# Two VectorE operations planned one unit later, and one copy out of PSUM shared by two engines

## The chip, the cores and the metric

The kernel runs on one NeuronCore of one Trainium2 chip. Times are device microseconds (us) of that core. Before the change the kernel takes 263.32 us, the median of 7 runs (263.03 to 264.03).

The engines are TensorE (PE in the profile; PEld are its weight loads), VectorE (DVE), ScalarE (ACT), GpSimd (POOL) and SyncE (SP, which here only issues DMAs). Each engine works through its own instructions strictly in order and waits at an instruction until what it needs has been signalled. PSUM is the matmul's output memory, in eight banks of 512 fp32 columns by 128 partitions.

## The reference

For each of 8 batches and 8 heads, with sequence 576 and head dimension 64:

```
q_s = exp(q) / sum over d of exp(q)          # softmax over the head dimension
k_s = exp(k) / sum over s of exp(k)          # softmax over the sequence
kv  = k_s^T v                                # 64 x 64 per head
x   = q_s kv                                 # heads side by side: 4608 tokens x 512
h   = x w_in                                 # 4608 x 2048
out = (h * sigmoid(h)) w_out                 # 4608 x 512, fp32
```

The inputs are q, k, v (8 x 8 x 576 x 64) and w_in (512 x 2048), w_out (2048 x 512), all fp32. The reference also subtracts a maximum before each exp and adds 1e-9 to each sum.

## The kernel before

**Tiling.** The 4608 tokens are cut into nine chunks `t` of 512 tokens. Attention is done batch by batch (576 tokens). As 576 is 512 and 64 more, batch 0 fills chunk 0 and the first 64 columns of chunk 1, batch 1 gives the other 448 columns of chunk 1 and the start of chunk 2, and so on. `pieces(t)` says which columns of which batch make up a chunk; for chunk 1 the columns that are still to be made begin at 64, hence the shapes 128x448 and 128x896 (two of them) in the profile.

**Attention of a batch `b`.** ScalarE takes the exp of q (`exp_q`, line 108) and of k (`exp_k`, line 113), in two calls each, one per two pairs of heads. VectorE sums exp(q) over the head dimension and takes the reciprocal (`qsum`, lines 154 to 158: with an argument `gs` it sums one group of heads per call, and the reciprocal follows the second). GpSimd or VectorE multiplies by it (`qnorm`, line 163). The normalised q is transposed, by TensorE for batches 0 and 1 and by a DMA on SP's queue (`q_transpose`, line 173) from batch 2 on. `vcast` turns v into bf16 with a column of ones (line 91 or 89). `kv` (line 195) multiplies k and v on TensorE into banks 6 and 7, `kvcopy` (lines 206 and 208) normalises the result on VectorE into `kvn`, and `xt` makes x transposed from it: `xt_mm` (line 234) writes banks 6 and 7 (bank `6 + s` for the head `s` of a pair of heads), and `xt_evac` copies both banks to the fp16 tile `XTS[t % 2]`, by one instruction on the engine that it is given. `xt(t, 0)` and `xt(t, 1)` use the same two banks one after the other. The helper `copy` (lines 89 and 91) records all copies.

**First matmul (x w_in).** Chunk 0 is done plainly. In chunk 1, eight of sixteen blocks of 128 features, and in chunks 2 to 8 all of them, are done in groups with seven half-size products in place of eight (Strassen's scheme in Winograd's form): `group(t, g, i)` for i in the order 1, 2, 6, 5, 7, 4, 3, line 377. Each product needs sums or differences of halves of the weights (`ws_op`, line 328, on VectorE, into `WS`) or of x (`xs_op`, line 338, on VectorE, into `XS1` to `XS4`). After products 1, 6 and 7 the banks 0 and 1 are copied out as `h` (`group_snap`, line 89 or 91), and after 2, 7 and 3 VectorE adds the other pair of banks to such a copy (`group_add`, line 355). That other pair is 6 and 7 in chunk 1, and 2 and 3 in later chunks. Products 2, 5 and 3 write it: 5 begins anew in the banks after the add of 2 has read them, and 3 adds to what 5 left after the add of 7 has read them. `group_silu` (line 361) on ScalarE makes `GT`, the input of the second matmul.

**Second matmul (g w_out).** Chunk 0 is done plainly (`mm2_plain`, line 414, into banks 2 to 5). Chunks 1 to 8 use the same seven-product scheme (`prod`, line 477), with `T1` to `T4` made once from w_out by `t_op` (line 461) on VectorE, and with sums of `GT` made for each chunk by `s_op` (line 451) on VectorE. `s_op(t, i, f0, f1)` does the part of the blocks f0 to f1.

**Order.** The order is written out by hand. The list `units` holds TensorE's work, one piece after the other; `plan(u, f)` puts `f` ahead of unit `u`. What is emitted ahead of a unit, or by the unit itself after its matmuls (a snapshot, an add), enters each engine's own queue in this order, so an operation moved past a unit moves past what that unit emits for the same engine. Functions planned for the same unit are emitted in the order of the `plan` calls. Units that the change touches:

- `b1` is the first unit after chunk 0's first matmul. Units `b1` to `b1 + 8` are `mm2_plain(0, 0)` to `mm2_plain(0, 8)`. Then, to `b1 + 22`, seven products of `group(1, 1, i)` and the other seven `mm2_plain` mix: product 1 is unit `b1 + 9`, product 2 is `b1 + 11`, product 6 is `b1 + 12`, product 5 is `b1 + 14`, product 7 is `b1 + 16`, product 4 is `b1 + 19` and product 3 is `b1 + 21`. Units `b1 + 23` to `b1 + 30` are plain blocks of chunk 1 (`mm1`, line 285). Batch 2's attention is planned between these: its q by `exp_q(2, ...)`, `qsum(2, ...)` and `qnorm(2, ...)`, then the k-v product at `b1 + 25` and x at `b1 + 27` and `b1 + 29`.
- `begin[NCH]` is the first unit of the last chunk's second matmul. The 28 units before it mix the last chunk's first matmul with chunk 7's second one; unit `begin[NCH] - 7` is product 7 of the last group, `- 6` a product of chunk 7's second matmul, `- 2` product 3 of the last group.

Of the kernel before, what the change touches and what calls it, by code (L numbers as in the profile page):

```python
# [17 lines left out]
def kernel(  # L18
# [9 lines left out]
    nc = tc.nc  # L28
# [9 lines left out]
    TCH = 512  # L38
    HT = TCH // 2
    HN = DM // 2  # L40
    NCH = NT // TCH
# [24 lines left out]
    XTS = [glob.tile([128, NC, S], FP16, name=f"XT{i}") for i in range(2)]  # L66
# [7 lines left out]
    PS = ps.tile([128, 8, 512], FP32, name="PS")  # L74
# [12 lines left out]
    def copy(eng, o, i):  # L87
        if eng is nc.scalar:
            eng.copy(out=o, in_=i)  # L89
        else:  # L90
            eng.tensor_copy(o, i)  # L91
# [10 lines left out]
    def half(t, cc):  # L102
        return t[:, :, cc * 128:(cc + 1) * 128].rearrange("p j (g d) -> p j g d", d=D)

    def exp_q(b, cc, g0=0, g1=2):
        if "eq" not in st[b]:
            st[b]["eq"] = ap.tile([128, J, NG * D], BF16, name="eq")
        nc.scalar.activation(  # L108
            out=half(st[b]["eq"], cc)[:, :, g0:g1], in_=jgd(b, "qt", cc)[:, :, g0:g1], func=ACT.Exp
        )  # L110
# [34 lines left out]
    def new_zq(b):  # L145
        if "zq" not in st[b]:
            st[b]["zq"] = ap.tile([128, 2, J, 2], FP32, name="zq", bufs=2)
            st[b]["rzq"] = ap.tile([128, 2, J, 2], FP32, name="rzq", bufs=2)

    def qsum(b, cc, gs=None):  # L150
        new_zq(b)
        z, e = st[b]["zq"][:, cc], half(st[b]["eq"], cc)
        if gs is None:
            nc.vector.reduce_sum(out=z, in_=e, axis=AX.X)  # L154
        else:
            nc.vector.reduce_sum(out=z[:, :, gs], in_=e[:, :, gs, :], axis=AX.X)  # L156
        if gs != 0:
            nc.vector.reciprocal(out=st[b]["rzq"][:, cc], in_=z)  # L158

    def qnorm(b, cc, eng):  # L160
        e = half(st[b]["eq"], cc)
        r = st[b]["rzq"][:, cc]
        eng.tensor_tensor(  # L163
            out=e, in0=e, in1=r[:, :, :, None].to_broadcast([128, J, 2, D]), op=ALU.mult
        )
# [49 lines left out]
    def kv_both(b):  # L215
        kv(b, 0)
        kv(b, 1)
        kvcopy(b)

    def pieces(t):  # L220
        a, e = (S, 2 * TCH) if t == 1 else (t * TCH, (t + 1) * TCH)
        got = []
        while a < e:
            b, col = divmod(a, S)
            n = min(S - col, e - a)
            got.append((b, col, n, a - t * TCH))
            a += n
        return got

    def xt_mm(b, cc, col, n, bank, dst):  # L230
        for r in range(2):
            for s in range(2):
                h = slice(s * 64, (s + 1) * 64)
                nc.tensor.matmul(  # L234
                    out=PS[r * 64:(r + 1) * 64, bank + s, dst:dst + n],
                    lhsT=kvn[b % 3][h, cc, r, :],
                    rhs=st[b]["qT"][h, col // P:(col + n) // P, cc, r * 64:(r + 1) * 64],
                )

    def xt_evac(t, cc, bank, d0, d1, o0, eng):  # L240
        o = XTS[t % 2][:, 2 * cc:2 * cc + 2, o0:o0 + d1 - d0]
        copy(eng, o, PS[:, bank:bank + 2, d0:d1])

    def xt(t, cc, eng=nc.scalar):
        got = pieces(t)
        for b, col, n, dst in got:
            xt_mm(b, cc, col, n, 6, dst)
        xt_evac(t, cc, 6, got[0][3], TCH, got[0][3], eng)


    def silu(t, fb, i, o, w):
# [68 lines left out]
    def ws_op(i, g):  # L320
        w, f0, f1 = WS[g], 4 * g + 8, 4 * g
        in0, in1, op = {
            1: (wa(0, f1), wa(1, f1), ALU.add),
            2: (w[0], wa(0, f0), ALU.subtract),
            3: (wa(0, f0), wa(0, f1), ALU.subtract),
            4: (wa(1, f0), w[1], ALU.subtract),
        }[i]
        nc.vector.tensor_tensor(out=w[i - 1], in0=in0, in1=in1, op=op)

    def xs_op(t, i):  # L330
        x = [xs[:, :, 0:width(t)] for xs in XS4]
        in0, in1 = {
            1: (xb(t, 0, 1), xb(t, 0, 0)),
            2: (xb(t, 1, 1), x[0]),
            3: (xb(t, 1, 1), xb(t, 0, 1)),
            4: (xb(t, 1, 0), x[1]),
        }[i]
        nc.vector.tensor_tensor(out=x[i - 1], in0=in0, in1=in1, op=ALU.subtract)
# [100 lines left out]
    def blk(t, kh, th):  # L439
        return GTS[t % 2][:, kh * HF:(kh + 1) * HF, th * HT:(th + 1) * HT]  # L440

    def s_op(t, i, f0=0, f1=HF):
        in0, in1, op = {
            1: (blk(t, 0, 1), blk(t, 1, 1), ALU.add),
            2: (SS[1], blk(t, 0, 0), ALU.subtract),
            3: (blk(t, 0, 0), blk(t, 0, 1), ALU.subtract),
            4: (blk(t, 1, 0), SS[2], ALU.subtract),
        }[i]
        f = slice(f0, f1)
        o = blk(t, 0, 1) if i == 3 else SS[i]  # L450
        nc.vector.tensor_tensor(out=o[:, f], in0=in0[:, f], in1=in1[:, f], op=op)

    def t_op(i, eng, f0=0, f1=HF):
        o, in0, in1 = {
            1: (T1, B12, B11),
            2: (T2, B22, T1),
            3: (T3, B22, B12),
            4: (T4, B21, T2),
        }[i]
        f = slice(f0, f1)  # L460
        eng.tensor_tensor(out=o[:, f], in0=in0[:, f], in1=in1[:, f], op=ALU.subtract)
# [161 lines left out]
    def plan(u, f):  # L623
        at.setdefault(u, []).append(f)
# [7 lines left out]
    begin = {1: len(units)}  # L632
# [25 lines left out]
    def full(t):  # L658
# [27 lines left out]
        plan(u + 17, lambda: q_transpose(b))  # L686
        plan(u + 15, lambda: kv_both(b))
        plan(u + 22, lambda: xt(t + 1, 0, nc.vector))
        plan(u + 27, lambda: xt(t + 1, 1))
        plan(u, lambda: (xs_op(t, 1), xs_op(t, 2), xs_op(t, 3), xs_op(t, 4)))  # L690

    for t in range(2, NCH):
        if t < B - 1:
            full(t)
            continue
        begin[t] = u = len(units)
        bs = b_units(t - 1, ORDER)
        gs = [lambda t=t, g=g, i=i: group(t, g, i) for g in (1, 0) for i in ORDER]
        plan(u + 2, lambda t=t: s_op(t - 1, 1))
        plan(u + 4, lambda t=t: s_op(t - 1, 2))  # L700
        plan(u + 5, lambda t=t: s_op(t - 1, 3))
        plan(u + 21, lambda t=t: s_op(t - 1, 4))
        for x in 2 * four_pairs:
            units.append({"b": bs, "g": gs}[x].pop(0))
            if x == "g" and len(gs) % 7 == 0:
                later = 1 if t == NCH - 1 and not gs else 3
                f0 = 12 if gs else 8
                plan(len(units) - 1 + later, lambda t=t, f0=f0: group_silu(t, 1, f0, 1))
        assert not (bs or gs)
        plan(u, lambda t=t: (xs_op(t, 1), xs_op(t, 2), xs_op(t, 3), xs_op(t, 4)))  # L710
        if t < NCH - 1:
            plan(u + 23, lambda t=t: xt(t + 1, 0, nc.vector))
            plan(u + 26, lambda t=t: xt(t + 1, 1))
# [2 lines left out]
    begin[NCH] = len(units)  # L716
    last = NCH - 1
    plan(begin[NCH] - 11, lambda: s_op(last, 1, 4, 8))
    plan(begin[NCH] - 7, lambda: s_op(last, 2, 4, 8))
    plan(begin[NCH], lambda: (s_op(last, 1, 0, 4), s_op(last, 2, 0, 4), s_op(last, 3)))  # L720
    plan(begin[NCH] + 6, lambda: s_op(last, 4))

# [48 lines left out]
    b1 = begin[1]  # L771
# [16 lines left out]
    plan(b1 + 5, lambda: (vcast(1, 1, nc.scalar, 0, 1), vcast(1, 1, nc.vector, 1, 2)))  # L788
    plan(b1 + 6, lambda: (trcopy(1, 1, 0, 5, 0, nc.scalar), trcopy(1, 1, 5, J, 1)))
    plan(b1 + 7, lambda: kv_both(1))  # L790
    plan(b1 + 8, lambda: xt(1, 0))
    plan(b1 + 9, lambda: xt(1, 1))

    plan(b1 + 3, lambda: (ws_op(1, 1), ws_op(2, 1)))
    plan(b1 + 4, lambda: ws_op(3, 1))
    plan(b1 + 6, lambda: ws_op(4, 1))
    plan(b1 + 8, lambda: t_op(1, nc.vector))
    plan(b1 + 10, lambda: (xs_op(1, 1), ws_op(1, 0)))
    plan(b1 + 10, lambda: (xs_op(1, 2), xs_op(1, 3), xs_op(1, 4)))
    plan(b1 + 10, lambda: exp_q(2, 0))  # L800
    plan(b1 + 11, lambda: (qsum(2, 0, 0), qsum(2, 0, 1), qnorm(2, 0, nc.gpsimd)))
    plan(b1 + 13, lambda: exp_q(2, 1))
    plan(b1 + 14, lambda: exp_k(2, 0))
    plan(b1 + 14, lambda: (qsum(2, 1, 0), qsum(2, 1, 1), qnorm(2, 1, nc.gpsimd)))
# [56 lines left out]
```

## Time and profile before

| | |
|---|---|
| median of 7 runs | 263.32 us |
| profiled execution, whole | 264.22 us |
| its span, first to last instruction | 262.4 us |
| mean granted TensorE clock | 0.997 |
| TensorE matmuls busy | 251.6 us, 96% of the span |
| VectorE busy | 208.9 us, 80% |
| ScalarE busy | 187.5 us, 71% |
| GpSimd busy | 65.6 us, 25% |
| HBM traffic | 36.70 MB read, 9.44 MB written |

The profile is one execution, recorded by the hardware profiler. A row of the timeline gives the start from the span's start, the length, the engine, the line of the program and the operation with output and input; in brackets, where there is one, the idle time of the engine before it and what ended it. An instruction's recorded end reaches a little into the next one of the same engine, since their parts overlap; matmuls follow each other before the earlier one's recorded end, a 512-column one 0.216 us after its predecessor's start. The chain of waits goes back from the last instruction to whatever released each step.

In this program chunk 0's first matmul ends at about 32.5 us, units `b1` to `b1 + 30` take until about 64 us, seven stretches of about 26 us for chunks 2 to 8 follow, and the second matmul of the last chunk begins at about 245 us.

### The profile page before, as it was taken

What the parts mean: (1) busy time and instruction counts of PE and PEld (TensorE: products, weight loads), DVE (VectorE), ACT (ScalarE), POOL (GpSimd) and SP (SyncE); (2) the same over time, 40 slices, a digit from 0 to 9 for tenths busy, and PEclk for the clock granted to TensorE, in tenths of its full rate; (3) what the DMA queues carried; (4) which work ended last, traced back from release to release, by engine and by line L of the source; (5) the groups of instructions that cost most, each with busy time, mean ns of one, the idle gap of its engine ahead of it and who ended that gap; (6) DMA issues with size and microseconds to landing.
All of it is one profiled execution on the core that took longest, in us unless ns stands there. A gap on an engine that the chain in (4) does not pass through costs nothing.

```text
span 262.4 us, 6409 instructions
## 1 busy us (share of the span) xinstructions
PE 251.6 (96%) x2732; PEld 203.2 (77%) x2732; DVE 208.9 (80%) x268; ACT 187.5 (71%) x212; POOL 65.6 (25%) x63
## 2 busy tenths in 40 slices
PE   8799899799999999999999999999999999999992
PEld 3367656465888888888888888888888888888881
DVE  2867797999897999799979997999798548855832
ACT  4765887698996699669966995699574748484610
POOL 1643691370270306030603060306000000000003
PEclk9999999999999999999999999999999999999998
DMA  6999999659999587857784879540434003400624
GB/s 248 338 188 296 300 326 330 242 97 354 332 332 215 159 213 253 163 167 170 295 202 133 207 254 181 155 98 2 90 71 92 2 0 72 91 2 1 139 64 120
DMA packets 35964, 45.89 MB, mean 175 GB/s; under 512 B 16208, under 2 KB 21008, under 8 KB 35936
## 3 DMA queue, kind: packets, MB, share of 16 engines
q1 hardware_dynamic: 29568, 33.69, 47.1%
q0 software_dynamic: 6128, 11.60, 17.2%
q8 instruction: 21, 0.34, 0.5%
q10 hardware_dynamic: 240, 0.20, 0.2%
q14 instruction: 7, 0.06, 0.1%
HBM read 36.70 MB, written 9.44 MB: 176 GB/s over the span
## 4 chain that ended last, share of the span: by engine, by line
PE 83%; DMA 5%; issue 4%; POOL 2%; ACT 2%; DVE 2%; POOLq 0%; ACTq 0%
PE PS L477 36%; PE PS L377 34%; DMA qt<-in_q_dram 5%; PE PS L414 5%; PE PS L285 2%; PE PS L234 2%; PE PS L195 2%; POOL W L554 1%; PE PS L267 1%; POOL out_dram L740 1%; ACT eq L108 1%; DVE zq L156 1%; ACT sg L256 0%; PE PS L181 0%; DVE h L355 0%
## 5 line engine op out<-in xcount | busy, mean ns | idle before, releaser
L355 DVE TENSOR_TENSOR h<-PS,h 128x1024 f32<-128x1024 f32 (+1 forms) x45 | 53.9, 1198 | 12.2 <-ACT h L89 6.3
L477 PEld LDWEIGHTS <-GT 128*128 128x128 f16 x512 | 49.6, 98 | 6.9 <-issue 1.2
L377 PEld LDWEIGHTS <-WS 128*128 128x128 f16 x480 | 46.8, 98 | 7.9 <-issue 2.3
L477 PE MATMUL PS<-W,GT 128*128 128x256 f16 x384 | 49.1, 273 | 0.0
L377 PE MATMUL PS<-XS,WS 128*128 128x256 f16 (+1 forms) x360 | 46.3, 272 | 1.5 <-DVE h L355 1.5
L361 ACT ACTIVATE GT<-h 128x1024 f16<-128x1024 f32 (+1 forms) x45 | 46.1, 1047 | 0.3 <-DVE h L355 0.3
L89 ACT COPY h<-PS 128x1024 f32<-128x1024 f32 (+1 forms) x35 | 35.1, 1004 | 14.7 <-PE PS L377 14.3
L477 PEld LDWEIGHTS <-S 128*128 128x128 f16 x384 | 37.1, 98 | 5.2 <-issue 1.0
L163 POOL TENSOR_TENSOR eq<-eq,rzq 128x1152 bf16<-128x1152 bf16 x13 | 27.5, 2116 | 54.6 <-DVE rzq L158 51.9
L377 PEld LDWEIGHTS <-W 128*128 128x128 f16 x360 | 34.7, 98 | 4.7 <-issue 0.2
L477 PE MATMUL PS<-T,S 128*128 128x256 f16 x256 | 32.7, 273 | 0.0
L377 PE MATMUL PS<-XT,W 128*128 128x256 f16 (+1 forms) x240 | 29.5, 272 | 0.0
L361 ACT ACTIVATE GT<-PS 128x1024 f16<-128x1024 f32 (+1 forms) x15 | 15.3, 1017 | 18.9 <-PE PS L377 18.9
L91 POOL CAST vaug<-vt 128x1152 bf16<-128x1152 f32 x12 | 14.8, 1240 | 45.1 <-DMA vt<-in_v_dram 37.1
L108 ACT ACTIVATE eq<-qt 128x1152 bf16<-128x1152 f32 (+1 forms) x18 | 19.1, 1059 | 3.5 <-DMA qt<-in_q_dram 3.4
L740 POOL DMA_DIRECT2D out_dram<-ow x5 | 2.7, 546 | 72.5 <-DVE ow L725 72.5
L113 ACT ACTIVATE ek<-kt 128x1152 bf16<-128x1152 f32 x16 | 18.4, 1154 | 1.5 <-DMA kt<-in_k_dram 1.5
L154 DVE TENSOR_REDUCE zq<-eq 128x18 f32<-128x1152 bf16 x12 | 16.1, 1345 | 4.0 <-ACT eq L108 4.0
L267 PE MATMUL PS<-XT,W 128*128 128x288 f16 x128 | 16.2, 286 | 1.1 <-DVE GT L257 0.8
L477 PE MATMUL PS<-W,S 128*128 128x256 f16 x128 | 16.5, 273 | 0.0
L497 DVE SCALAR_TENSOR_TENSOR ow<-PS,sc 128x512 f32<-128x512 f32 x7 | 4.8, 692 | 14.5 <-ACT sc L493 14.5
L267 PEld LDWEIGHTS <-W 128*128 128x128 f16 x128 | 12.4, 98 | 4.9 <-issue 1.2
(79 smaller groups left out, 347.7 us busy)
## 6 DMA issues: line engine op xcount, KB each, us to landing
out_dram<-ow SPq DMA_DIRECT2D x64, 128.0 KB, 2.4
qt<-in_q_dram SPq DMA_DIRECT2D x12, 576.0 KB, 4.6
kt<-in_k_dram SPq DMA_DIRECT2D x12, 576.0 KB, 5.7
vt<-in_v_dram SPq DMA_DIRECT2D x12, 576.0 KB, 5.5
qt<-in_q_dram POOLq DMA_DIRECT2D x4, 576.0 KB, 10.8
kt<-in_k_dram POOLq DMA_DIRECT2D x4, 576.0 KB, 13.8
vt<-in_v_dram POOLq DMA_DIRECT2D x4, 576.0 KB, 12.6
W<-in_moe_w_out_dram POOLq DMA_DIRECT2D x4, 512.0 KB, 14.9
```

The costliest lines, as they stand in the source:

```text
L89: eng.copy(out=o, in_=i)
L91: eng.tensor_copy(o, i)
L108: nc.scalar.activation(out=half(st[b]["eq"], cc)[:, :, g0:g1], in_=jgd(b, "qt", cc)[:, :, g0:g1], func=ACT.Exp)
L113: nc.scalar.activation(out=half(ek, cc), in_=jgd(b, "kt", cc), func=ACT.Exp)
L154: nc.vector.reduce_sum(out=z, in_=e, axis=AX.X)
L163: eng.tensor_tensor(out=e, in0=e, in1=r[:, :, :, None].to_broadcast([128, J, 2, D]), op=ALU.mult)
L267: nc.tensor.matmul(out=PS[:, WIDE[fb] + n, 0:S // 2], lhsT=W1[:, c, fb * 128:(fb + 1) * 128], rhs=XTS[0][:, c, n * (S // 2):(n + 1) * (S / ...
L355: nc.vector.tensor_tensor(out=four(t, i), in0=group_bank(t, True), in1=four(t, i), op=ALU.add)
L361: nc.scalar.activation(out=group_out(t, f, n), in_=x, func=ACT.Silu, scale=1.0 / XS)
L377: nc.tensor.matmul(out=PS[:, bank + p // 2, (p % 2) * HT:(p % 2) * HT + width(t)], lhsT=a[:, c, p * 128:(p + 1) * 128], rhs=bb[:, c, 0:wid ...
L414: nc.tensor.matmul(out=PS[:, 2 + tb, :], lhsT=GTS[t % 2][:, fc, tb * 128:(tb + 1) * 128], rhs=W2[:, fc, :], start=(fc == 0), stop=(fc == N ...
L477: nc.tensor.matmul(out=PS[:, bank, m * HN:(m + 1) * HN], lhsT=a[:, fc, m * 128:(m + 1) * 128], rhs=bb[:, fc, :], start=(first and fc == 0) ...
```

## The change

There are three edits.

- `xt(1, 0)`, batch 1's x for the first two pairs of heads, is copied out of PSUM by two instructions: ScalarE takes bank 6 and VectorE bank 7, 128x448 each, where ScalarE took both, 128x896, in one. `t_op(1)`, the first sum of w_out's quarters (`T1`), was planned for `b1 + 8` after `xt(1, 0)` and is now planned for `b1 + 9`; in VectorE's queue it comes after the new copy.
- `qsum(2, 0, 0)` and `qsum(2, 0, 1)` on VectorE, with the reciprocal, and the following `qnorm(2, 0)` on GpSimd are planned for `b1 + 12` in place of `b1 + 11`. Unit `b1 + 11` is product 2, which emits its add for VectorE; the sums come behind it now.
- `s_op(last, 2, 4, 8)` is planned for `begin[NCH] - 6` in place of `- 7`. Unit `begin[NCH] - 7` is product 7 of the last group, which emits its add for VectorE; the subtraction comes behind it now.

```diff
@@ -245,7 +245,12 @@
         got = pieces(t)
         for b, col, n, dst in got:
             xt_mm(b, cc, col, n, 6, dst)
-        xt_evac(t, cc, 6, got[0][3], TCH, got[0][3], eng)
+        if eng is None:
+            o0 = got[0][3]
+            for s, e in enumerate((nc.scalar, nc.vector)):
+                copy(e, XTS[t % 2][:, 2 * cc + s, o0:TCH], PS[:, 6 + s, o0:TCH])
+        else:
+            xt_evac(t, cc, 6, got[0][3], TCH, got[0][3], eng)
@@ -716,7 +721,7 @@
     begin[NCH] = len(units)
     last = NCH - 1
     plan(begin[NCH] - 11, lambda: s_op(last, 1, 4, 8))
-    plan(begin[NCH] - 7, lambda: s_op(last, 2, 4, 8))
+    plan(begin[NCH] - 6, lambda: s_op(last, 2, 4, 8))
@@ -788,17 +793,16 @@
     plan(b1 + 7, lambda: kv_both(1))
-    plan(b1 + 8, lambda: xt(1, 0))
-    plan(b1 + 9, lambda: xt(1, 1))
+    plan(b1 + 8, lambda: xt(1, 0, None))
+    plan(b1 + 9, lambda: (t_op(1, nc.vector), xt(1, 1)))
 
     plan(b1 + 3, lambda: (ws_op(1, 1), ws_op(2, 1)))
     plan(b1 + 4, lambda: ws_op(3, 1))
     plan(b1 + 6, lambda: ws_op(4, 1))
-    plan(b1 + 8, lambda: t_op(1, nc.vector))
     plan(b1 + 10, lambda: (xs_op(1, 1), ws_op(1, 0)))
     plan(b1 + 10, lambda: (xs_op(1, 2), xs_op(1, 3), xs_op(1, 4)))
     plan(b1 + 10, lambda: exp_q(2, 0))
-    plan(b1 + 11, lambda: (qsum(2, 0, 0), qsum(2, 0, 1), qnorm(2, 0, nc.gpsimd)))
+    plan(b1 + 12, lambda: (qsum(2, 0, 0), qsum(2, 0, 1), qnorm(2, 0, nc.gpsimd)))
     plan(b1 + 13, lambda: exp_q(2, 1))
```

## The prediction

> **What bounds the kernel now.** I read the page first, then the list of who waited for whom in the stage of batch 1 (39 to 66 us), then the chain of waits and the timeline there, and the timeline of the last 25 us. On the page the thing to see is that TensorE holds the chain; only time during which TensorE stands still is to be won.
>
> ```profile
> span 262.4 us, 6409 instructions
> ...
> PE 251.6 (96%) x2732; PEld 203.2 (77%) x2732; DVE 208.9 (80%) x268; ACT 187.5 (71%) x212; POOL 65.6 (25%) x63
> ...
> PE 83%; DMA 5%; issue 4%; POOL 2%; ACT 2%; DVE 2%; POOLq 0%; ACTq 0%
> ```
>
> The list of TensorE's waits from 39 to 66 us has one row, of waits, times and the longest:
>
> ```profile
> PE PS L377 <- DVE h L355: 1.5, 1, 1.5
> ```
>
> The chain of waits (start, length, what) says how VectorE's add came to be late: ScalarE's exp of batch 2's q, then the sums `qsum` over it on VectorE, then the reciprocal, and only then the add that frees banks 6 and 7.
>
> ```profile
> 44.89 1.18 ACT eq L108
> 46.07 0.02 issue
> 46.09 1.43 DVE zq L156 x2
> 47.52 0.02 issue
> 47.54 0.27 DVE rzq L158
> 47.80 0.96 DVE h L355
> 48.76 0.04 issue
> 48.80 0.93 PE PS L377 x8
> ```
>
> In the timeline (start, length, engine, line), note that the matmuls before the stall start at 46.23, and that an fp16 subtraction on VectorE which meets a running GpSimd operation takes far longer than its kind elsewhere:
>
> ```profile
> 46.23 1.03 PE L414 MATMUL PS<-W,GT 128*128 128x512 f16 x4
> ...
> 47.72 1.03 DVE L355 TENSOR_TENSOR h<-PS,h 128x896 f32<-128x896 f32 x1
> 47.99 2.11 POOL L163 TENSOR_TENSOR eq<-eq,rzq 128x1152 bf16<-128x1152 bf16 x1 [7.26 <-DVE rzq L158]
> ...
> 48.66 1.98 DVE L328 TENSOR_TENSOR WS<-WS,W 128x1024 f16<-128x1024 f16 x1
> ...
> 59.53 0.49 DVE L208 TENSOR_TENSOR kvn<-PS,rz 128x128 bf16<-128x128 f32 x2
> ...
> 60.14 0.41 PE L234 MATMUL PS<-qT,kvn 64*64 64x128 bf16 x8
> ```
>
> The tail's timeline has a smaller case of the same kind: the add at 241.96 is queued behind a subtraction nobody needs yet, and the matmuls at 243.23 wait for it.
>
> ```profile
> 241.35 0.69 DVE L451 TENSOR_TENSOR S<-S,GT 128x1024 f16<-128x1024 f16 x1
> 241.96 1.22 DVE L355 TENSOR_TENSOR h<-PS,h 128x1024 f32<-128x1024 f32 x1
> ...
> 243.23 1.03 PE L377 MATMUL PS<-XT,WS 128*128 128x256 f16 x8
> ```
>
> **Part 1, the split copy and the first sum of W2.** Removed: one ScalarE copy of 128x896 from PSUM (41.78, 0.91). Added: 128x448 on ScalarE and 128x448 on VectorE. ScalarE's 128x448 activations from PSUM took 0.54 (line 296). For VectorE no row has this shape: the 128x512 cast of x took 0.69, the 128x512 bf16 copy 0.42. I take 0.62, the cast's row less 64 columns at the slope to the 128x1024 cast (1.22 less 0.69 over 512). Both halves then end by 42.40, with 0.69 by 42.47. The next matmuls in these banks, the second head pair's x, have their first weight load at 42.63 and start at 42.74, just after the old copy's end at 42.69. So TensorE gains 0.11 and no more: what is late next is the mm2 matmuls ahead of them (41.67, four at 0.216). Either bound of the copy leaves that unchanged, and a loss would need a copy over 0.85.
>
> The subtraction T1 (1.21) moves from 41.21 to behind VectorE's copy, so it runs 42.33 to 43.54. Behind it on VectorE follow the first `xs_op` (0.39), `ws_op(1, 0)` (0.68) and three more `xs_op`, each starting 0.07 before its predecessor's recorded end, as in the trace: the second `xs_op`, which product 6 needs, ends at 44.78; product 6 wants it at 45.46 - 0.11 = 45.35. The last ends at 45.38. VectorE stood idle 0.30, 0.39 and 0.98 in this stretch before, and that idle time hides copy and T1. Without it product 6 would come late by up to the 0.62 of the copy. That the readers of x now wait for two engines I bound by 0 and the 0.05 us that a release takes in these rows; 0.57 us of cover for product 6 make it nothing.
>
> The Trainium skill, "VectorE: DVE Perf Modes", in the section on the TRN2 errata, speaks against such a split: each instruction pays a fixed cost, so one large tile is better than several. Its formulas give, as an estimate, 0.52 us for ScalarE's half and 0.59 us for VectorE's; the page's objection is about engine time, and the sum would stay as it is.
>
> **Part 2, `qsum` one unit later.** It puts the add of product 2 (`group_add(1, 0)`) ahead of two reductions and a reciprocal. It needs product 2, which starts at 44.70 - 0.11 = 44.59 and lasts 0.93, and ScalarE's snapshot, done by 44.9. So the add runs from 45.57 to 46.60. Product 5 could follow the mm2 matmuls at 46.23 + 0.87 = 47.10 in the old time, 46.99 in the new one; the add is 0.39 ahead of that. The stall goes: 48.80 - 47.10 = 1.70 us. Together with part 1, TensorE is 1.81 early.
>
> What is queued behind: reductions at 46.50, reciprocal at 47.95 (old 47.54), `ws_op(2, 0)` 0.18 later at 48.13, as the next operation followed the reciprocal before. GpSimd's `qnorm` starts 0.45 after the reciprocal's start in the trace, so at 48.40. Before, `ws_op(2, 0)` came into a running qnorm and ended at 50.64, which is 0.54 after the qnorm's end at 50.10. Now it comes 0.27 ahead. T2's subtraction shows the other side: it held the first `vcast` on GpSimd, 2.15 us against 1.15 for the second. I therefore take 0.68 for `ws_op`, ended 48.81, with the qnorm held until then. The held cast ran 1.02 after T2's end, 0.13 under its usual time, so the qnorm ends at 48.81 + 1.98 = 50.79. The other bound is `ws_op` held once more until 51.05; it is the first rival.
>
> The Trainium skill, "SBUF — State Buffer", in the section on its two separate sides, says that VectorE and GpSimd share a port pair and that the operation that starts first keeps it for the whole instruction; the rows agree (1.98 against 0.68). By the page alone the winner of 48.13 against 48.40 is VectorE, and the sum stays.
>
> Then the second reductions (48.74), reciprocal (50.18), and the second qnorm (50.75 to 52.87, old end 54.53): 1.66 early. The add of product 7 starts at 50.54, after ScalarE's snapshot, and is done 1.1 before product 3 wants its banks at 52.74. T2 waits for the qnorm as before and ends 1.08 after it, at 53.95; all that follows on VectorE and GpSimd is 1.66 early, while TensorE is 1.81 early. The casts end at 56.07 and the second half of the new k·v product wants them at about 56.35: nothing. The normalised kv is ready at 60.02 - 1.66 = 58.36, plus 0.06 to start; TensorE wants it at 60.14 - 1.81 = 58.33: 0.09 given back.
>
> Loads: nothing that issues a DMA from SP or GpSimd is moved past another; transposed q and batch 3's loads start earlier because their releasers do. What TensorE or ScalarE now meets earlier has landed: the last W2 block (issued 36.72, landing in 9.6) at 46.3 against use at 49.4, k of batch 2 at 47.8 and 49.3 against 48.2 and 50.4, v at 50.8 and 52.2 against a first cast at 52.9. The transposed q, 4.7 from issue, arrives at 57.6 against 58.4. ScalarE's own chain, table load of 1.28 included, moves with its releasers.
>
> **Part 3, `s_op(last, 2, 4, 8)` one unit later.** The add of product 7 starts at about 241.28 instead of 241.96 and ends at 242.50. TensorE could start product 3 at 242.15 + 0.87 = 243.02 and started at 243.23: 0.21 won. The subtraction (0.69) now lies between that add and the scaling at 243.09, which keeps its time; its result is read at 246.75, over 3 us later. The last add follows product 3, and the last silu follows that add by 0.03, so the tail moves as one. If that chain did not move along, its silu, ready at 246.67 and wanted at 246.71, would take up to the 0.21 back.
>
> **Sum.** 0.11 + 1.70 - 0.09 + 0.21 = 1.93 us. From 64 to 243 us TensorE stands on the chain with its other engines released by it, so the shift is carried. The profiled execution took 264.22 (span 262.4 and 1.82 around it), which gives 262.29; it stands 0.90 above the median of 263.32, so the median becomes 261.4.
>
> **Rivals.** (a) GpSimd's qnorm gets ahead of `ws_op(2, 0)`. For it: the pair met in that order before, and only 0.27 us of lead, put together from two differences, decides it. Price: `ws_op` ends at 50.51 + 0.54 = 51.05 instead of 50.64, the second reciprocal and qnorm are 0.41 later than before, so are T2, the casts and the normalised kv: 60.43 + 0.06 against 60.14, a loss of 0.35. Less 0.21 in the tail it is 0.14 slower than before: 263.5. It decides from the point where the qnorm starts before 48.13; all of 1.81 is gone then. Against it: nothing that ws_op reads is written later than the reciprocal.
> (b) The order holds but the held qnorm pays its start again, 0.45 and 2.12 after `ws_op`: it ends at 51.38, the second at 53.50, VectorE's chain is only 1.03 early, and the batch-2 x 1.09. Gain 1.09 + 0.21 = 1.30: 262.0. Against it: the held cast's 1.02.
> (c) The stall is not the add's: another operand of product 5 holds it. Then only 0.11 and 0.21 remain: 263.0. Against it: the add ends at 48.75 and the matmul starts at 48.80, and product 5's own operands were written before 45.2.
>
> **How the numbers follow.** My sum 0.70, (b) 0.14, (a) 0.10, (c) 0.03, and 0.03 for a loss I don't see. About 0.2%, 0.53 us, is what a measurement of this kernel tells from no change. My sum and (b) are faster by more: 0.84. (a) and (c) mostly lie within: 0.11. Slower by more: 0.05. The range takes my sum with 0.6 below, for the terms and the scatter of the runs (263.03 to 264.03), and reaches over (b) with 0.7 above it, leaving (a), (c) and the unseen out: 260.8 to 262.7.
>
> **What would show it.** Product 5 starts near 47.0 with no wait for line 355; `ws_op(2, 0)` at 0.7 us and the first batch-2 qnorm at about 2.4; x of batch 2 at 58.4; product 3's matmuls in the tail without a gap. The prediction is wrong if `ws_op(2, 0)` again takes about 2 us or more, if product 6 waits for an `xs_op`, or if the lead at 58 us is lost before 240.

## The result and the profile after

The changed kernel takes 261.58 us (median of 12 runs, 261.27 to 262.46) against 263.42 for the kernel before (median of 31). The ratio is 0.9933, with a 95% interval of 0.9922 to 0.9944: 1.76 us won (1.5 to 2.1). The prediction on record is 261.4.

The page of the kernel after, the lines that answer to those shown of before (line numbers of the changed file are 5 higher behind the edit of `xt`):

```profile
span 260.4 us, 6414 instructions
...
PE 251.1 (96%) x2732; PEld 203.2 (78%) x2732; DVE 208.0 (80%) x269; ACT 187.0 (72%) x212; POOL 65.8 (25%) x63
...
PE 80%; DMA 5%; DVE 5%; issue 4%; POOL 2%; ACT 1%; POOLq 0%; ACTq 0%; DVEq 0%
```

TensorE's work is what it was: the same 2732 matmuls. The span is 2.0 shorter because TensorE stands still for less of it. VectorE's share of the chain has gone up, from 2% to 5%, although the add it was waited for no longer stops anything; where that 5% lies is shown below.

The list of TensorE's waits from 39 to 66 us, which had one row before (line 355, 1.5 us), is empty. The timeline of the kernel after, in the same stretch (start, length, engine, line, operation):

```profile
45.49 1.09 DVE L360 TENSOR_TENSOR h<-PS,h 128x896 f32<-128x896 f32 x1 [0.25 <-PE PS L382]
45.99 1.03 PE L419 MATMUL PS<-W,GT 128*128 128x512 f16 x4
46.85 0.93 PE L382 MATMUL PS<-XS,WS 128*128 128x224 f16 x8
47.93 0.27 DVE L158 RECIPROCAL rzq<-zq 128x18 f32<-128x18 f32 x1
48.12 0.63 DVE L333 TENSOR_TENSOR WS<-WS,W 128x1024 f16<-128x1024 f16 x1
48.38 4.41 POOL L163 TENSOR_TENSOR eq<-eq,rzq 128x1152 bf16<-128x1152 bf16 x2 [7.81 <-DVE rzq L158]
```

Read three things. The add now runs straight behind product 2 and is done 0.27 us before product 5 starts at 46.85. Product 5 starts at its slot: the matmuls of chunk 0's second matmul (`mm2`) ahead of it start at 45.99, and their four follow each other in 0.86. And `ws_op(2, 0)` starts 0.26 ahead of GpSimd's first `qnorm` and takes 0.63, where it took 1.98 before; the two qnorms take 4.41 together, 2.33 and 2.11, the first one stretched.

The chain of waits of the kernel after shows what replaced the stall. VectorE's chain from the second sums over T2 to the normalised kv of batch 2 is now what batch 2's x waits for:

```profile
51.39 2.49 DVE T L466
53.88 1.00 DVE h L360
54.88 0.60 DVE ow L434
55.48 1.60 DVE T L466
57.07 0.60 DVE WS L333
57.67 0.10 DVE rz L206
57.78 0.02 issue
57.80 0.50 DVE kvn L208 x2
58.30 0.04 issue
58.34 0.41 PE PS L234 x8
```

The list puts 5% of the span, some 13 us, down to this chain, but only 0.15 us of it is lost time: the eight matmuls ahead of 58.34 started at 56.58 and take 1.61 with the change to smaller matmuls (as 58.53 to 60.14 before), so TensorE was free at 58.19. In the tail the order of the two VectorE operations is turned round, and product 3 follows without a gap (0.88 behind the matmuls before it, which start at 240.35, against 1.08 before):

```profile
239.43 1.22 DVE L360 TENSOR_TENSOR h<-PS,h 128x1024 f32<-128x1024 f32 x1
240.56 0.68 DVE L456 TENSOR_TENSOR S<-S,GT 128x1024 f16<-128x1024 f16 x1
...
241.23 1.04 PE L382 MATMUL PS<-XT,WS 128*128 128x256 f16 x8
```

The two profiled executions differ by 0.14 us already at 41 us, ahead of everything that was changed: chunk 0's first matmul stalls a little differently from execution to execution (its matmuls stood 0.36 us for a load of w_in in the one of before and not in the one after). So starts are compared here from one point on, the mm2 matmuls of unit `b1 + 8`, just ahead of batch 1's second x. Every start in the table is from the timeline of that kernel; the last column is the difference of the one before it to 18.47.

| kernel | unit `b1 + 8` | product 5 | batch 2's x | from unit to x | against before |
|---|---|---|---|---|---|
| before | 41.67 | 48.80 | 60.14 | 18.47 | |
| after | 41.53 | 46.85 | 58.34 | 16.81 | -1.66 |
| sums later, alone | 41.08 | 46.50 | 58.00 | 16.92 | -1.55 |
| split copy, alone | 40.89 | 48.24 | 59.58 | 18.69 | +0.22 |
| one more wait | 40.76 | 48.22 | 59.56 | 18.80 | +0.33 |
| T1 ahead of the copy | 41.41 | 47.10 | 58.59 | 17.18 | -1.29 |
| tail order, alone | 41.12 | 48.26 | 59.60 | 18.48 | +0.01 |
| two reciprocals more | 41.56 | 46.88 | 58.62 | 17.06 | -1.41 |
| four reciprocals more | 41.71 | 47.03 | 60.64 | 18.93 | +0.46 |
| `ws_op(3, 0)` later | 40.66 | 45.98 | 57.33 | 16.67 | -1.80 |

From batch 2's x to the last chunk's tail the lead is kept to the hundredth: 60.14 to 242.15 before and 58.34 to 240.35 after are both 182.01 us.

### The profile page after: what moved, and what is told of

Its sections match the earlier page's. It is cut to its first block, busy times and chain, and to the rows that moved or that the text cites. A ratio compares the mean times of both kernels' runs of the same rounds, so it can differ in the third digit from the quotient of the medians.

```text
span 260.4 us, 6414 instructions
## 1 busy us (share of the span) xinstructions
PE 251.1 (96%) x2732; PEld 203.2 (78%) x2732; DVE 208.0 (80%) x269; ACT 187.0 (72%) x212; POOL 65.8 (25%) x63
## 4 chain that ended last, share of the span: by engine, by line
PE 80%; DMA 5%; DVE 5%; issue 4%; POOL 2%; ACT 1%; POOLq 0%; ACTq 0%; DVEq 0%
PE PS L482 37%; PE PS L382 34%; DMA qt<-in_q_dram 5%; PE PS L419 3%; PE PS L234 2%; PE PS L195 2%; DVE T L466 2%; POOL W L559 1%; PE PS L290 1%; PE PS L272 1%; DVE zq L156 1%; DVE h L360 1%; POOL out_dram L745 1%; ACT sg L261 0%; DVE WS L333 0%
```

## The experiments

**1. The sums alone.** The kernel before with this one edit:

```diff
-    plan(b1 + 11, lambda: (qsum(2, 0, 0), qsum(2, 0, 1), qnorm(2, 0, nc.gpsimd)))
+    plan(b1 + 12, lambda: (qsum(2, 0, 0), qsum(2, 0, 1), qnorm(2, 0, nc.gpsimd)))
```

> The kernel before with qsum(2, 0) one unit later and nothing else. My theory: the stall of 1.70 us ahead of product 5 goes; TensorE has no wait for VectorE's add, product 5 follows the mm2 matmuls at 47.10. VectorE's chain from product 2's add to the normalised kv of batch 2 then gives 0.15 back ahead of batch 2's x, as in the changed kernel. Gain 1.55 us, ratio 0.994. Rival (the split copy is worth more than its 0.11, since it brings the whole x earlier): gain of 1.2 or less, ratio 0.9955 or more, with a wait left ahead of product 5 or of product 6.

Measured: 262.07 us against 263.35, ratio 0.9956 (0.9943 to 0.9969). The list of TensorE's waits from 39 to 66 us is empty here too. The add runs ahead of the sums, and product 5 starts 0.86 behind the mm2 matmuls at 45.64:

```profile
45.14 1.09 DVE L355 TENSOR_TENSOR h<-PS,h 128x896 f32<-128x896 f32 x1 [0.63 <-PE PS L377]
46.15 1.41 DVE L156 TENSOR_REDUCE zq<-eq 128x9 f32<-128x576 bf16 x2
...
45.64 1.03 PE L414 MATMUL PS<-W,GT 128*128 128x512 f16 x4
46.50 0.93 PE L377 MATMUL PS<-XS,WS 128*128 128x224 f16 x8
```

From unit to x it wins 1.55, the number expected. By the runs it is 1.16 us (0.8 to 1.5); the trace's 1.55 lies just beyond that interval. The stall was the order on VectorE, and most of the gain is this edit; 0.6 us lie between the ratio of this kernel and that of the changed one, whose intervals overlap, and the trace gives 0.11 and 0.20 of it to the other two edits.

**2. The split copy alone**, the changed kernel with both orders put back:

```diff
-    plan(begin[NCH] - 6, lambda: s_op(last, 2, 4, 8))
+    plan(begin[NCH] - 7, lambda: s_op(last, 2, 4, 8))
...
-    plan(b1 + 12, lambda: (qsum(2, 0, 0), qsum(2, 0, 1), qnorm(2, 0, nc.gpsimd)))
+    plan(b1 + 11, lambda: (qsum(2, 0, 0), qsum(2, 0, 1), qnorm(2, 0, nc.gpsimd)))
```

> The changed kernel with both orders put back, so only the split copy and T1 behind it. My theory: the second x matmuls start at their weight load, 0.11 us earlier, ScalarE's chain to the exp and so the late add move by as much, the stall ahead of product 5 stays at 1.70 us from slot to start: gain 0.11, ratio 0.9996, not to be told from no change by the time. Rival (T1 and the copy push the xs operations so far that product 6 waits): product 6 starts more than 0.05 us after its slot and the time is 0.2 us or more above before.

Measured: 263.98 against 263.35, ratio 1.0026 (1.0009 to 1.0042): slower by 0.7 us (0.2 to 1.1). My theory said 0.11 faster; the rival had the sign, but for a reason that the trace doesn't show. Product 6 does not wait (44.58, 0.76 behind product 2's start, as before), so the rival falls. The second x does start 0.11 earlier, counted from the unit. But the stall ahead of product 5 grows from 1.70 to 2.02. ScalarE's timeline in this kernel:

```profile
42.30 0.91 ACT L89 CAST XT<-PS 128x896 f16<-128x896 f32 x1 [0.76 <-PE PS L234]
43.53 0.91 ACT L89 COPY h<-PS 128x896 f32<-128x896 f32 x1 [0.32 <-issue]
44.33 1.17 ACT L108 ACTIVATE eq<-qt 128x1152 bf16<-128x1152 f32 x1
```

and in the kernel before:

```profile
43.17 0.91 ACT L89 CAST XT<-PS 128x896 f16<-128x896 f32 x1 [0.48 <-PE PS L234]
44.09 0.91 ACT L89 COPY h<-PS 128x896 f32<-128x896 f32 x1
44.89 1.17 ACT L108 ACTIVATE eq<-qt 128x1152 bf16<-128x1152 f32 x1
```

The snapshot of product 1 (`h`) starts 0.32 us after the engine is free, with "issue" as what ended the idle time: nothing in the profile that it waited for. The exp stands behind it, the sums wait for the exp, the add stands behind the sums, and product 5 waits for the add. So -0.11 and +0.33 give the table's +0.22, which lies at the lower end of what the runs give. The same idle time of 0.32 to 0.33 us is in all six kernels with the split copy, in the changed one too, where the sums stand behind the add and it costs nothing.

**3. One more wait, without the split.** The trace also keeps the rows of semaphores, which the views shown here leave out. In them an instruction of ScalarE that has two waits stands as two: a semaphore instruction that waits for one thing, and behind it the instruction itself, which waits for the other. Ahead of the snapshot the kernels with the split copy differ from the one before in one such row: the second copy of x, which waited for TensorE alone, now waits for TensorE and VectorE. So the kernel before was given that second wait and nothing else. VectorE sets an element to zero that ScalarE's copy then overwrites:

```diff
-    plan(b1 + 9, lambda: xt(1, 1))
+    plan(b1 + 9, lambda: (nc.vector.memset(XTS[1][:, 2, TCH - 1:TCH], 0.0), xt(1, 1)))
```

> The kernel before with one element of batch 1's second x set to zero by VectorE behind T1, ahead of ScalarE's copy that writes it anyway: ScalarE's second copy of x now waits for VectorE besides TensorE, and VectorE is done 0.6 us before it could start. Nothing else moves. My theory for the 0.33 us by which ScalarE's snapshot of product 1 is late wherever the first copy of x is split: it comes from that second wait on the copy ahead of it. Then the snapshot is 0.33 late here too, with no work that it waits for, the exp, the sums, the late add and product 5 follow, and the stall ahead of product 5 is 2.0 in place of 1.70: 0.33 us slower than before, ratio 1.001. Rival (it comes from the split copy itself, its form or its length): the snapshot follows the copy at once as before, the stall is 1.70, ratio 1.000.

Measured: 263.57 against 263.41, ratio 1.001 (1.0 to 1.0021). The memset on VectorE, and ScalarE's timeline:

```profile
41.47 0.06 DVE L792 MEMSET XT<- 128x1 f16 x1
...
42.27 0.91 ACT L89 CAST XT<-PS 128x896 f16<-128x896 f32 x1 [0.48 <-PE PS L234]
43.50 0.91 ACT L89 COPY h<-PS 128x896 f32<-128x896 f32 x1 [0.33 <-issue]
```

The idle time is back, with the full-size copy and no change in its form, and from unit to x the kernel is 0.33 slower; the runs agree (0 to 0.6), but by themselves could not tell it from nothing. VectorE's memset had ended at 41.53, 0.7 ahead of the copy's start, so the wait never held anything. The second wait on an instruction costs the next instruction 0.33 us here; that it comes from the wait and not from the split is shown. The snapshot has two waits itself, for product 1 and for GpSimd, and none for VectorE, so the memset can't have held it. Its semaphore row, the wait for product 1, is passed 0.03 us after product 1's recorded end in both kernels (44.03 before, 43.13 here), 0.05 ahead of the copy's end; the snapshot starts 0.06 behind that row before and 0.37 behind it here. Why the second wait delays the instruction behind and not the one that has it isn't settled: the copy itself still starts 0.05 behind the matmuls. The first copy of x has had two waits in the kernel before too, but after it ScalarE idles anyway.

**4. T1 ahead of the copy.** The changed kernel with T1 in its old place:

```diff
-    plan(b1 + 8, lambda: xt(1, 0, None))
-    plan(b1 + 9, lambda: (t_op(1, nc.vector), xt(1, 1)))
+    plan(b1 + 8, lambda: (t_op(1, nc.vector), xt(1, 0, None)))
+    plan(b1 + 9, lambda: xt(1, 1))
```

> The changed kernel with T1 ahead of the split copy, as T1 stood before. My theory: VectorE's half of the copy starts when T1 lets go, 0.54 us later, ends about 0.55 us later; the second x matmuls start 0.38 later than in the changed kernel, and so do product 2, its add and the chain on VectorE: 0.38 us slower than the changed kernel, 262.0, ratio to before about 0.9945. Rival (there is slack behind it that takes the delay up): as the changed kernel, 0.993.

Measured: 262.18, ratio 0.9957 (0.9943 to 0.9971). From unit to x it is 0.37 slower than the changed kernel. TensorE's timeline shows the loss where it arises: the second x matmuls stretch from 0.38 to 0.76, since the half that goes to bank 6 can start and the other half waits for VectorE's copy out of bank 7.

```profile
41.41 1.04 PE L419 MATMUL PS<-W,GT 128*128 128x512 f16 x4
42.38 0.76 PE L234 MATMUL PS<-qT,kvn 64*64 64x448 bf16 x4
43.06 0.94 PE L382 MATMUL PS<-XT,W 128*128 128x224 f16 x8
```

So the split copy pays only with T1 put behind it (and, by experiment 2, only with the sums moved as well); no slack takes the delay up.

**5. The tail order alone**, on the kernel before:

```diff
-    plan(begin[NCH] - 7, lambda: s_op(last, 2, 4, 8))
+    plan(begin[NCH] - 6, lambda: s_op(last, 2, 4, 8))
```

> The kernel before with s_op(last, 2, 4, 8) one unit later and nothing else. My theory: product 3's matmuls of the last group follow without the gap of 0.21 us and everything after moves with them: gain 0.21 in the trace from there to the end, ratio 0.9992. Rival (the silu that follows the last add is fixed by something else): product 3 starts 0.21 earlier, but the last chunk's second matmul stalls as much later; gain 0.

Measured: 263.20 against 263.35, ratio 1.0004 (0.9986 to 1.0023), which can't tell 0.2 us. In the trace product 3 starts 0.87 behind the matmuls before it (241.74 and 242.61; 1.08 before), and the last chunk's second matmul 2.62 behind them (244.36) where it was 2.82 (242.15 and 244.97). The gap is gone and does not come back as a stall of that matmul; its worth in time is shown by the trace alone.

**6. The port, two reciprocals more.** Rival (a) of the prediction turns on whether `ws_op(2, 0)` or the qnorm comes first. The changed kernel with extra VectorE work between the reciprocal and `ws_op`:

```diff
+    def again():
+        for i in range(2):
+            nc.vector.reciprocal(out=st[1]["rzq"][:, i], in_=st[2]["zq"][:, 0])
+
-    plan(b1 + 12, lambda: (qsum(2, 0, 0), qsum(2, 0, 1), qnorm(2, 0, nc.gpsimd)))
+    plan(b1 + 12, lambda: (qsum(2, 0, 0), qsum(2, 0, 1), qnorm(2, 0, nc.gpsimd), again()))
```

> The changed kernel with the reciprocal of the first sums taken two more times, into an unused place, so that ws_op(2, 0) comes 0.38 us later, just behind GpSimd's start of qnorm and not ahead of it. It computes nothing new. My theory (the operation that comes first keeps the other out): ws_op(2, 0) is held until 0.54 us after the qnorm's end, 2.3 us later than in the changed kernel in all; the qnorm is not held and takes 2.11; the second qnorm, T2, the casts and the normalised kv of batch 2 come about 2.1 us later: 263.7, ratio to before 1.000 to 1.002. Rival (the two engines do not shut each other out; ws_op was slow before for another reason): only the 0.38 us of work counts, 261.8 to 262.0, ratio 0.994 to 0.995, with ws_op at about 0.7 us.

Measured: 261.85, ratio 0.9939 (0.9919 to 0.9959). A miss of the design: the two reciprocals took 0.25 and not 0.38, and `ws_op` still came first, at 48.40 against 48.42.

```profile
48.40 0.63 DVE L333 TENSOR_TENSOR WS<-WS,W 128x1024 f16<-128x1024 f16 x1
48.42 4.66 POOL L163 TENSOR_TENSOR eq<-eq,rzq 128x1152 bf16<-128x1152 bf16 x2 [7.49 <-DVE rzq L158]
```

It says something nevertheless. A lead of 0.02 us is enough here for VectorE to run at full pace, and the first qnorm now takes 2.58: its end is 1.97 after `ws_op`'s, as in the changed kernel (1.96, from 48.75 to 50.71).

**7. The port, four reciprocals more**, the same edit with `range(4)` and `i % 2`.

> The changed kernel with the reciprocal taken four more times, into an unused place, so that ws_op(2, 0) comes 0.2 us or more behind GpSimd's start of qnorm; with two more it still came 0.02 ahead. It computes nothing new. My theory (the operation that comes first keeps the other out): ws_op(2, 0) ends 0.54 us after the qnorm's end, about 2.3 us later than in the changed kernel; the qnorm takes 2.11 and not 2.33; product 3 of batch 1's group waits for VectorE's add, and batch 2's x comes about 2.1 us later: 263.7, ratio to before 1.000 to 1.002. Rival (no such exclusion): ws_op takes about 0.7, only 0.5 us of work counts, 262.1, ratio 0.995.

Measured: 263.78 against 263.41, ratio 1.0019 (1.0009 to 1.0029). Now the qnorm comes first, by 0.28, and everything turns:

```profile
48.56 2.11 POOL L163 TENSOR_TENSOR eq<-eq,rzq 128x1152 bf16<-128x1152 bf16 x1 [7.49 <-DVE rzq L807]
48.84 2.38 DVE L333 TENSOR_TENSOR WS<-WS,W 128x1024 f16<-128x1024 f16 x1
```

`ws_op` ends 0.55 after the qnorm. The list of TensorE's waits from 39 to 66 us in this kernel:

```profile
PE PS L382 <- DVE h L360: 0.9, 1, 0.9
PE PS L195 <- POOL vaug L91: 0.6, 1, 0.6
PE PS L234 <- DVE kvn L208: 0.2, 1, 0.2
```

Product 3, the k·v product and x of batch 2 all wait; from unit to x it is 2.12 slower than the changed kernel, and the whole gain is lost with 0.46 more (the tail gives 0.20 of it back). The time of the four reciprocals is not what counts: the qnorm starts 6.85 behind the unit in both kernels, and `ws_op` ends when the qnorm lets it. Half a microsecond in the start of `ws_op` (6.59 behind unit `b1 + 8` in the changed kernel, 7.13 here) separates a kernel that is 0.7% faster than before from one that is 0.2% slower. The rule of the Trainium skill, "SBUF — State Buffer", section on the two separate sides, that the operation which starts first keeps the shared port pair for its whole instruction, holds in both directions here.

**8. Taking the new wait away.** The new bound is VectorE's chain ahead of the normalised kv. `ws_op(3, 0)` stands in it and is first read in chunk 2:

```diff
-    plan(b1 + 24, lambda: (t_op(4, nc.vector), ws_op(3, 0)))
+    plan(b1 + 24, lambda: t_op(4, nc.vector))
+    plan(begin[2] + 1, lambda: ws_op(3, 0))
```

> The changed kernel with ws_op(3, 0), which is first read in chunk 2, moved from ahead of the normalisation of batch 2's kv to the first units of chunk 2, where VectorE was idle for 1.05 us. My theory: the normalised kv is the last to arrive at batch 2's x, by 0.15 us; now it is ready 0.60 us earlier, the x matmuls start at their slot, and 0.15 us is won to the end: 261.4, ratio 0.9927. Rival (the copy of x or a matmul behind it is the next to be late, or ws_op at its new place delays product 2's add): the gap moves and the time is that of the changed kernel, 0.9933, or up to 0.4 above it.

Measured: 261.38 (4 runs, 261.21 to 261.51), ratio 0.9918 (0.9905 to 0.9931). Its timeline:

```profile
55.71 1.69 PE L290 MATMUL PS<-XT,W 128*128 128x448 f16 x8
56.33 0.49 DVE L208 TENSOR_TENSOR kvn<-PS,rz 128x128 bf16<-128x128 f32 x2
57.33 0.41 PE L234 MATMUL PS<-qT,kvn 64*64 64x128 bf16 x8
...
62.20 0.68 DVE L333 TENSOR_TENSOR WS<-W 128x1024 f16<-128x1024 f16 x1
```

The normalised kv is ready at 56.82, half a microsecond ahead of its use, x starts at its slot (1.62 behind 55.71), and from unit to x 0.14 is won over the changed kernel. The moved operation lies in VectorE's idle time at 62.2. It is the fastest kernel of the study; that it beats the changed one is shown by the trace, as the two intervals of the runs overlap.

## Why the prediction was right, point by point

**The sum.** Predicted 0.11 + 1.70 - 0.09 + 0.21 = 1.93. In the traces: 0.11 at the second x (42.50 - 41.53 against 42.74 - 41.67 is 0.10, to rounding), product 5 1.81 earlier counted from the unit (7.13 against 5.32), 0.15 given back at batch 2's x, 0.20 in the tail: 1.86. The runs give 1.76 (1.5 to 2.1), and the median of 261.58 stands 0.2 above the forecast of 261.4, inside the range of 260.8 to 262.7.

**Part 1.** The copies took 0.53 on ScalarE and 0.62 on VectorE (0.54 and 0.62 expected; 0.52 and 0.59 estimated from the page), the cap of 0.11 by the mm2 matmuls held, and product 6 was not late. One step was wrong: that the new waits cost 0 to 0.05 us. The prediction looked for them at the readers of x, which were not late. The wait that cost something stands on ScalarE's second copy, which the prediction doesn't name, and made the snapshot of product 1 0.33 late (experiments 2 and 3): it was not done by 44.9, but by 45.21 in the prediction's frame (45.07 in the trace, whose unit `b1 + 8` stands 0.14 earlier). In the changed kernel the add's own wait for product 2 hides it: the snapshot ended at 45.07, product 2 at 45.38. That it cost nothing was luck; no step of the prediction had foreseen it. Without the moved sums, part 1 is a loss of 0.22 by the trace. The fixed cost of an extra instruction, against which the page cited there speaks (of operations that read SBUF; its table has a fixed term for PSUM too), was not what told.

**Part 2.** The order of events came as written. The add took 1.09 and not 1.03 and started 0.06 later than reckoned against the unit, so the reciprocal came 0.12 later in the same frame; `ws_op` made up 0.05 with 0.63. The held qnorm ended 1.96 after `ws_op`, for 1.98. Of this, 0.06 arrives at the normalised kv, and that is the difference between 0.09 and 0.15 given back. The casts and the loads held nothing, as said.

**Part 3.** 0.20 for 0.21, and the tail moved as one.

**Rival (a)** did not happen, by a lead of 0.26 us (0.27 reckoned), but experiment 7 made it happen: 0.46 lost by batch 2's x where 0.35 were priced, and the kernel slower than before by 0.2%. Its chance of 1 in 10 rested on that lead; in experiment 6 a lead of 0.02 was enough. **Rival (b)**, that the held qnorm pays its whole start again, is excluded by 1.96 and 1.97 us from `ws_op`'s end to its end. **Rival (c)** is excluded by experiment 1.

## What to carry to other kernels

A short stall of the bound engine is often an order on another one: look what stands in that engine's queue ahead of the operation that releases it, and whether that is needed sooner. When such an operation is moved, check what it will now meet on a resource that two engines share; here half a microsecond decided between 0.7% faster and 0.2% slower. After the gain, the chain of waits names the next operation to move, even where only a tenth of a microsecond is lost.

## What was not expected of the hardware

An instruction of ScalarE that was given a second wait, on something finished 0.7 us earlier, started on time, but the instruction behind it started 0.33 us after the engine was free, with no work that it waited for (experiment 3; also in the six kernels with the split copy: 0.32 to 0.33, and in none of the other three). A dependency that never holds anything can so cost a third of a microsecond. Whether that holds for other engines, or needs the two waits which the second instruction has as well, no run here shows.

That VectorE's fp16 subtraction and GpSimd's multiply keep each other out was expected; how little decides it was not. It goes in both directions, in one case by a recorded lead of 0.02 us: 0.63 or 2.38 us for the one, 2.58 or 2.11 for the other. The one held ended 0.55 (`ws_op`) or 1.97 us (the qnorm) after the other's end, nearly its whole length, and shows in the timeline as a longer instruction, not as idle time.
